# Token mix of the last 64 tokens of two batches on column halves of the array, and scores on the full array

## The chip, the cores and the metric

The kernel runs on one core of one Trainium2 chip. The metric is device microseconds of that core for one launch. Before the change the median of three runs is 381.34 us (381.15 to 381.44).

A short guide to the names: TensorE (PE in the profile; PEld is its weight load) multiplies a stationary operand `lhsT` with a moving operand `rhs` into PSUM. VectorE (DVE), ScalarE (ACT) and GpSimd (POOL) work element by element. Each engine takes its own instructions in program order and waits for others by semaphores.

## The reference

Eight batches of 576 tokens, 8 heads of 64 columns. Attention uses keys and values that are means over 8 neighbouring tokens, so there are 72 keys a head. A residual MLP follows, whose first half mixes the tokens of a batch with one 576 x 576 matrix.

```python
k_p = k.reshape(B, H, Sp, pool, D).mean(axis=3)          # Sp = 72, pool = 8
v_p = v.reshape(B, H, Sp, pool, D).mean(axis=3)
scores = scale * np.matmul(q, k_p.transpose(0, 1, 3, 2))  # 576 x 72 a head
attn = softmax(scores)                                    # exp, divided by its sum
attn_out = np.matmul(attn, v_p)
# ... heads side by side: x is (8, 576, 512)
a1 = alpha1 * x + beta1
tok = np.einsum('ts,bsd->btd', w_tok, a1)
u = x + lam * tok
a2 = alpha2 * u + beta2
ch = np.maximum(a2 @ w_ch1, 0.0) @ w_ch2                  # 512 -> 2048 -> 512
return u + lam * ch
```

## The kernel before

The 576 tokens of a batch are four chunks of 128 and a tail of 64. The tails of an even and an odd batch share one chunk `(b, 4)`: the even one in partitions 0 to 63, the odd one in 64 to 127. There are 36 chunks in all, and the MLP takes them in nine blocks of four. While block `n` runs its MLP, the attention and the token mix of batch `n + 1` are woven in: `todo` is a list of (position, action), sorted by position, where one step of the position is about one group of MLP matmuls.

Tiles in PSUM come from a pool of six (`gp`), with two more for the MLP's output:

```python
psA = ctx.enter_context(tc.tile_pool(name="psA", bufs=6, space=bass.MemoryType.PSUM))
psB = ctx.enter_context(tc.tile_pool(name="psB", bufs=2, space=bass.MemoryType.PSUM))

def gp(name):
    return psA.tile([P, 512], FP, tag="gp", name=name)
```

Keys and queries of two heads lie one above the other: head `2*hp` in partitions 0 to 63, head `2*hp + 1` in 64 to 127. The pooled keys are copied out of PSUM with one instruction:

```python
def att_K(b, u, copy):
    # ... matmuls into kp: 128 partitions x (2 pairs x 72 keys)
    copy(out=kpT_pool[u], in_=kp)
```

Scores of a pair, in two halves of 288 tokens. Each product contracts over 64 rows of the array; the two heads use its two halves. ScalarE takes the exponential of each into ET.

```python
def att_S(b, hp):
    st = st1[b]
    u, r = hp // 2, hp % 2
    for half in range(2):
        n0 = 288 * half
        both = [gp("ps_sc") for _ in range(2)]
        for hh in range(2):
            rows = slice(64 * hh, 64 * hh + 64)
            nc.tensor.matmul(out=both[hh][0:SPG, 0:288], lhsT=kpT_pool[u][rows, r, :],
                             rhs=st["qT"][u][rows, S * r + n0:S * r + n0 + 288])
        for hh in range(2):
            nc.scalar.activation(out=ET_pool[2 * r + hh][:, 64 + n0:64 + n0 + 288],
                                 in_=both[hh][0:SPG, 0:288],
                                 func=AF.Exp, bias=0.0, scale=0.125)
    # ...
```

`att_AV` multiplies ET with the pooled values (ps_av, five matmuls of 66 columns), and VectorE divides by the sums (`rec`, then x_tm). `att_X` scales x into the mix's operand xs:

```python
def att_X(b, h0, h1, eng=nc.vector):
    # ...
    eng.tensor_tensor(out=xs[:, 0:4, cols], in0=x[:, 0:4, cols],              # L388
                      in1=lamal_bc[:, cols]..., op=ALU.mult)
    p0 = 64 * (b % 2)
    eng.tensor_tensor(out=xs[p0:p0 + 64, 4, cols], in0=x[p0:p0 + 64, 4, cols],  # L392
                      in1=lamal_bc[p0:p0 + 64, cols], op=ALU.mult)
```

The token mix. A tail (`c == 4`) is computed like a full chunk: 128 output columns of which 64 are used, once for the even batch and once for the odd one.

```python
def mix_T(b, c, eng=nc.vector):
    key, s = chunk_of(b, c)
    p0, p1 = (0, P) if c < 4 else (64 * (b % 2), 64 * (b % 2) + 64)
    xs = xs_pool[b % 2]
    ps_tok = gp("ps_tok")
    t0 = P * c - 64 * (b % 2) if c == 4 else P * c
    for sc in range(5):
        kk, at = (P, sc) if sc < 4 else (P, 5) if b % 2 else (65, 4)
        nc.tensor.matmul(out=ps_tok, lhsT=wtT[0:kk, at, t0:t0 + P],
                         rhs=xs[0:kk, sc, :], start=(sc == 0), stop=(sc == 4))   # L422
    nc.vector.tensor_tensor(out=s["u"][p0:p1, :], in0=st1[b]["x"][p0:p1, c, :],  # L424
                            in1=ps_tok[p0:p1, 0:DM], op=ALU.add)
    eng.tensor_tensor(out=s["u_bf"][p0:p1, :], in0=s["u"][p0:p1, :],             # L426
                      in1=al2_bc[p0:p1, :], op=ALU.mult)
```

`mix_uT` (L437) then transposes u_bf on TensorE, and the MLP reads the result. The schedule of the attention of batch `b`, woven into block `b - 1`; GpSimd's casts and sums come first in it:

```python
def attention(b):
    late = b == 1
    todo = [(11.9 if late else -2.0, lambda: cast_rem(b, nc.gpsimd))]           # L107, L108
    for u in range(2):
        at = 10.0 + 4.8 * u if late else -1.0 + 6.6 * u
        todo.append((at, lambda u=u: cast_q(b, u, nc.gpsimd.tensor_copy)))      # L114
        todo.append((at + 0.1, lambda u=u: sum_k(b, u, nc.gpsimd)))             # L121, L122
        # ... att_F, att_V, att_Frem, att_K
    for h in range(8):
        at = 17.0 + 0.9 * h if late else 13.1 + 1.0 * h
        lag = 1.6 if late else 2.0
        if h % 2 == 0:
            todo.append((at, lambda h=h: att_S(b, h // 2)))
        todo.append((at + lag, lambda h=h: att_AV(b, h)))
        # ... att_X after every second head
    for c in range(5):
        at = 26.2 + 0.9 * c if late else 25.0 + c
        todo.append((at, lambda c=c: mix_T(b, c)))
        if c < 4 or b % 2:
            # ...
            todo.append((at + 1.8, lambda key=key: mix_uT(key)))
    return todo
```

In block 0 two of the MLP's output tiles (ps_ch2) are taken from the pool of six, and the tail of batch 0 is mixed at position 11.4 of that block.

Of the kernel before, what the change touches and what calls it, by code (L numbers as in the profile page):

```python
# [9 lines left out]
BF = mybir.dt.bfloat16  # L10
AF = mybir.ActivationFunctionType
ALU = mybir.AluOpType
AX = mybir.AxisListType

P = 128
SPG = 72
DM = 512
# [6 lines left out]
def kernel(  # L24
# [18 lines left out]
    nc = tc.nc  # L43
    ctx.enter_context(tc.manual_schedule())
    B, H, S, D = q.shape

    const = ctx.enter_context(tc.tile_pool(name="const", bufs=1))
# [4 lines left out]
    def gp(name):  # L52
        return psA.tile([P, 512], FP, tag="gp", name=name)
# [11 lines left out]
    st1 = {}  # L65
# [70 lines left out]
    al2_bc = const.tile([P, DM], FP, tag="al2_bc", name="al2_bc")  # L136
# [6 lines left out]
    start = const.tile([1, 2], FP, tag="start", name="start")  # L143
# [11 lines left out]
    for i, src in ((1, moe_alpha1), (0, moe_lam)):  # L155
        n = 65 if i in (0, 3) else 1
        nc.gpsimd.dma_start(out=vecs[0:n:64, i],
                            in_=src.unsqueeze(0).to_broadcast((1 + n // 65, DM)))
# [32 lines left out]
    vp1_pool, kpT_pool, ET_pool = [], [], []  # L191
    for i in range(4):
        t = const.tile([SPG, 2, 66], F16, tag=f"vp1_{i}", name=f"vp1_{i}")
        nc.vector.memset(t, 8.0)
        vp1_pool.append(t)
        if i < 2:
            kpT_pool.append(const.tile([P, 2, SPG], BF, tag=f"kpT_{i}", name=f"kpT_{i}"))
        t = const.tile([SPG, S + 128], F16, tag=f"ET_{i}", name=f"ET_{i}")
        nc.vector.memset(t[:, 0:64], 1.0)
        nc.vector.memset(t[:, 64 + S:], 1.0)  # L200
        ET_pool.append(t)
# [4 lines left out]
    xs_pool = [const.tile([P, 5, DM], BF, tag=f"xs_{i}", name=f"xs_{i}") for i in range(2)]  # L206
# [3 lines left out]
    wtT = const.tile([P, 6, 640], BF, tag="wtT", name="wtT")  # L210
# [112 lines left out]
    def att_K(b, u, copy):  # L323

        st = st1[b]
        ps_kp = gp("ps_kp")
        kp = ps_kp[:, 0:2 * SPG].rearrange("p (r g) -> p r g", g=SPG)
        for r in range(2):
            nc.tensor.matmul(out=kp[:, r, 0:64],
                             lhsT=st["k"][u][:, 2 * r:2 * r + 2].rearrange("p h d -> p (h d)"),  # L330
                             rhs=pool_main)
        nc.tensor.matmul(out=kp[:, :, 64:72], lhsT=st["rem"][1].rearrange("p h d -> p (h d)"),  # L332
                         rhs=pool_rem.rearrange("p (g u r) -> p u r g", r=2, u=2)[:, u])
        copy(out=kpT_pool[u], in_=kp)  # L334

    def att_V(b, hp):

# [4 lines left out]
        nc.vector.tensor_tensor(out=vp1_pool[hp][:, :, 0:64], in0=t[:, :, 0], in1=t[:, :, 1],  # L342
                                op=ALU.add)

    def att_S(b, hp):

        st = st1[b]
        u, r = hp // 2, hp % 2
        for half in range(2):
            n0 = 288 * half  # L350
            both = [gp("ps_sc") for _ in range(2)]
            for hh in range(2):
                rows = slice(64 * hh, 64 * hh + 64)
                nc.tensor.matmul(out=both[hh][0:SPG, 0:288], lhsT=kpT_pool[u][rows, r, :],  # L354
                                 rhs=st["qT"][u][rows, S * r + n0:S * r + n0 + 288])
            for hh in range(2):
                nc.scalar.activation(out=ET_pool[2 * r + hh][:, 64 + n0:64 + n0 + 288],  # L357
                                     in_=both[hh][0:SPG, 0:288],
                                     func=AF.Exp, bias=0.0, scale=0.125)
        for hh in range(2):  # L360
            st["ET"][2 * hp + hh] = ET_pool[2 * r + hh]

    def att_AV(b, h):
        st = st1[b]
        if "x" not in st:
            st["x"] = work.tile([P, 5, DM], FP, tag="x_tm", bufs=1, name="x_tm")
        hp, hh = h // 2, h % 2
        ET, vp1, x = st["ET"][h], vp1_pool[hp], st["x"]
        ps_av = gp("ps_av")
        av = ps_av[:, 0:5 * 66].rearrange("p (c x) -> p c x", x=66)  # L370
        for c in range(4):
            m0 = 64 + 64 * (hp % 2) + 128 * c
            nc.tensor.matmul(out=av[:, c, :], lhsT=ET[:, m0:m0 + 128],  # L373
                             rhs=vp1[:, hh, :])

        r0 = (64 if hp % 2 else 576) - 64 * (b % 2)
        nc.tensor.matmul(out=av[:, 4, :], lhsT=ET[:, r0:r0 + 128], rhs=vp1[:, hh, :])
        rec = work.tile([P, 5], FP, tag="rec", bufs=2, name="rec")
        nc.vector.reciprocal(out=rec, in_=av[:, :, 64:65])
        dd = D * h  # L380
        nc.vector.tensor_tensor(out=x[:, :, dd:dd + D], in0=av[:, :, 0:64],  # L381
                                in1=rec.unsqueeze(2).to_broadcast((P, 5, D)), op=ALU.mult)
# [16 lines left out]
    def chunk_of(b, c):  # L399
        key = (b, c) if c < 4 else (b - b % 2, 4)  # L400
        if key not in st2:
            st2[key] = {
                "u": work.tile([P, DM], FP, tag="u_sb", bufs=12, name="u_sb"),
                "u_bf": work.tile([P, DM], BF, tag="u_bf", bufs=4, name="u_bf"),
            }
        return key, st2[key]
# [6 lines left out]

    def mix_T(b, c, eng=nc.vector):
        key, s = chunk_of(b, c)
        p0, p1 = (0, P) if c < 4 else (64 * (b % 2), 64 * (b % 2) + 64)
        xs = xs_pool[b % 2]
        ps_tok = gp("ps_tok")
        t0 = P * c - 64 * (b % 2) if c == 4 else P * c
        for sc in range(5):  # L420
            kk, at = (P, sc) if sc < 4 else (P, 5) if b % 2 else (65, 4)
            nc.tensor.matmul(out=ps_tok, lhsT=wtT[0:kk, at, t0:t0 + P],  # L422
                             rhs=xs[0:kk, sc, :], start=(sc == 0), stop=(sc == 4))
        nc.vector.tensor_tensor(out=s["u"][p0:p1, :], in0=st1[b]["x"][p0:p1, c, :],  # L424
                                in1=ps_tok[p0:p1, 0:DM], op=ALU.add)
        eng.tensor_tensor(out=s["u_bf"][p0:p1, :], in0=s["u"][p0:p1, :],  # L426
                          in1=al2_bc[p0:p1, :], op=ALU.mult)

    def mix_uT(key):
        s = st2[key]  # L430
# [61 lines left out]
    for i, p0 in ((0, 64), (1, 0)):  # L492
        nc.vector.tensor_tensor(out=xs_pool[i][p0:p0 + 1, 4, :], in0=vecs[p0:p0 + 1, 3],
                                in1=vecs[p0:p0 + 1, 0], op=ALU.mult)
    cast_rem(0, nc.gpsimd, nc.vector.tensor_copy)
    att_Frem(0, (0,), nc.vector.tensor_copy)
    att_K(0, 0, nc.scalar.copy)
    for hp in range(2):
        att_S(0, hp)
    nc.vector.tensor_tensor(out=lamal_bc, in0=lamal_bc, in1=lam_bc, op=ALU.mult)  # L500
    load_wtok()
    att_V(0, 0)
# [16 lines left out]
    att_X(0, 2, 4)  # L519
    att_V(0, 2)  # L520
    att_V(0, 3)
    for hp in (2, 3):
        att_S(0, hp)
    att_AV(0, 4)
    att_AV(0, 5)
    setup_wtok(0, nc.scalar.copy)
    att_X(0, 4, 6, nc.gpsimd)
# [6 lines left out]
    setup_wtok(3, nc.scalar.copy)  # L534
    att_X(0, 6, 8)
    mix_T(0, 0, nc.gpsimd)
    setup_rowsum(2)
    setup_rowsum(3)
# [22 lines left out]
    def attention(b):  # L561


        late = b == 1
        todo = [(11.9 if late else -2.0, lambda: cast_rem(b, nc.gpsimd))]
# [3 lines that stand above are left out]
            todo.append((at + 0.1, lambda u=u: sum_k(b, u, nc.gpsimd)))  # L569
            for r in range(2):  # L570
                at = 12.7 + 4.6 * u + 1.6 * r if late else 2.7 + 6.6 * u + 2.4 * r
                hp = 2 * u + r
                todo.append((at, lambda hp=hp: att_F(b, hp)))
                todo.append((at + 0.5, lambda hp=hp: att_V(b, hp)))
                if r:
                    todo.append((at + 0.1, lambda u=u: att_Frem(b, (u,), nc.scalar.copy)))
                    todo.append((at + 0.4, lambda u=u: att_K(b, u, nc.vector.tensor_copy)))
        for h in range(8):
            at = 17.0 + 0.9 * h if late else 13.1 + 1.0 * h
            lag = 1.6 if late else 2.0  # L580
            if h % 2 == 0:
                todo.append((at, lambda h=h: att_S(b, h // 2)))
            todo.append((at + lag, lambda h=h: att_AV(b, h)))
            if h % 2:
                eng = nc.gpsimd if late and h < 5 else nc.vector
                todo.append((at + lag + 0.1, lambda h=h, eng=eng: att_X(b, h - 1, h + 1, eng)))
# [4 lines that stand above are left out]
                key = (b, c) if c < 4 else (b - 1, 4)  # L591
                todo.append((at + 1.8, lambda key=key: mix_uT(key)))
        return todo

    for n in range(NBLK):
        todo = []
        for j in range(0 if n else 4, NJ):
            todo.append((j, lambda j=j: mlp_A(n, j)))
        for m in range(4):
            for part in range(4):  # L600
                at = 16 + (4 * m + part if n else 4 * part + m)
# [9 lines left out]
        b = n + 1  # L611
        if b < B:
            todo += attention(b)
            if b + 1 < B:
                new_batch(b + 1)
                for u in range(2):
                    at = 20.0 + 0.2 * u if b == 1 else 0.4 + 1.0 * u
                    todo.append((at, lambda b=b, u=u: load_qk(b + 1, u)))
                    at = 22.0 + 0.2 * u if b == 1 else 5.8 + 6.6 * u
# [34 lines left out]
```

## Time and profile before

| | |
|---|---|
| time, median of three | 381.34 us |
| span of the profiled run | 379.6 us |
| mean granted TensorE clock | 0.995 |
| TensorE busy | 354.6 us, 93% |
| VectorE busy | 221.5 us, 58% |
| ScalarE busy | 184.5 us, 49% |
| GpSimd busy | 77.7 us, 20% |
| HBM | 38.04 MB read, 9.44 MB written |

How to read the lines that follow. A line of the page's shares gives busy time, share of the span and instructions of an engine. The chain is followed back from the last instruction to what released it, and shares say where its time lies. A line of the timeline gives the start and the length in microseconds of a run of like instructions, the engine, the line of the kernel, the operation, what is written from what, rows and columns of the array for a matmul ("64*72" is 64 rows, 72 columns), the shape, and how many; in brackets is the idle time of the engine before it and what ended it. Matmuls are pipelined: the next starts before the one before it has ended, so what one costs in a stream is the distance between starts.

### The profile page before, as it was taken

To read this page: it belongs to the slowest core of one execution; us is meant where nothing else is said; L and a number is where in the kernel's file an instruction comes from. 1 tells how busy PE (TensorE), PEld (TensorE's weight loads), DVE (VectorE), ACT (ScalarE), POOL (GpSimd) and SP (SyncE) were. 2 spreads that over 40 slices of the span, in tenths; PEclk is the share of its full clock that TensorE was granted. 3 is DMA by queue.
4 is the path that set the end of the run, shared out by engine and by line. 5 is a ranking of instruction groups with operands and counts; after the bars stand their busy time and mean duration, and the time that the engine had idled before them with its cause. 6 is when DMAs were issued, how large, how long until landed. Compare 5 with 4: busy or idle time off the path is not lost.

```text
span 379.6 us, 5854 instructions
## 1 busy us (share of the span) xinstructions
PE 354.6 (93%) x2241; PEld 185.7 (49%) x2283; DVE 221.5 (58%) x446; ACT 184.5 (49%) x380; POOL 77.7 (20%) x94
## 2 busy tenths in 40 slices
PE   2879999699999999999999999999999999999995
PEld 0365654245554555455545554555455544544542
DVE  4797756775596468736874688548754784011011
ACT  1574665117931693159415951586148603712710
POOL 7553432900700070007000700061000000000000
PEclk9999999989999999999999999999999999999999
DMA  8999999207631563147313732293110012002012
GB/s 201 223 200 214 262 238 253 49 29 242 154 90 58 169 173 90 57 139 201 90 57 121 219 92 56 75 264 86 40 50 1 3 54 57 0 29 83 1 48 65
DMA packets 34845, 43.02 MB, mean 113 GB/s; under 512 B 2360, under 2 KB 24956, under 8 KB 34816
## 3 DMA queue, kind: packets, MB, share of 16 engines
q1 hardware_dynamic: 31744, 37.76, 36.4%
q0 software_dynamic: 3072, 4.87, 7.3%
q8 instruction: 18, 0.29, 0.3%
q14 instruction: 11, 0.09, 0.1%
HBM read 38.04 MB, written 9.44 MB: 125 GB/s over the span
## 4 chain that ended last, share of the span: by engine, by line
PE 87%; DVE 7%; DMA 2%; issue 2%; POOL 1%; ACT 1%; POOLq 0%; DVEq 0%
PE ps_h L453 33%; PE ps_ch L471 32%; PE ps_tok L422 11%; PE ps_sc L354 3%; PE ps_uT L437 2%; DMA vecs<-in_moe_beta_dram 2%; PE ps_av L373 2%; PE ps_q L300 2%; DVE x_tm L381 1%; DVE v_u L340 1%; DVE xs L388 1%; DVE xs L392 1%; DVE u_sb L424 1%; DVE u_bf L426 1%; PE ps_bias L288 1%
## 5 line engine op out<-in xcount | busy, mean ns | idle before, releaser
L471 PE MATMUL ps_ch<-w,Hj 128*128 128x512 bf16 x555 | 137.7, 381 | 1.7 <-issue 0.8
L453 PE MATMUL ps_h<-u_fm,w 128*128 128x512 bf16 (+2 forms) x576 | 132.0, 374 | 0.9
L458 ACT ACTIVATE Hj<-ps_h,bias_cols 128x512 bf16<-128x512 f32 x144 | 97.9, 689 | 43.6 <-PE ps_h L453 42.7
L453 PEld LDWEIGHTS <-w 128*128 128x128 bf16 x592 | 63.6, 114 | 50.9 <-issue 1.6
L471 PEld LDWEIGHTS <-Hj 128*128 128x128 bf16 x576 | 51.3, 98 | 54.5 <-issue 6.8
L439 ACT COPY u_fm<-ps_uT 128x512 bf16<-128x512 bf16 x36 | 21.1, 585 | 99.7 <-PE ps_uT L437 99.6
L476 DVE TENSOR_TENSOR u_sb<-u_sb,ps_ch 128x512 f32<-128x512 f32 x36 | 24.5, 683 | 55.7 <-PE ps_ch L471 55.5
L422 PE MATMUL ps_tok<-xs,wtT 128*128 128x512 bf16 (+1 forms) x196 | 50.1, 385 | 3.7 <-DVE xs L388 3.2
L357 ACT ACTIVATE ET<-ps_sc 72x288 f16<-72x288 f32 x128 | 41.4, 412 | 19.2 <-PE ps_sc L354 19.0
L340 DVE TENSOR_TENSOR v_u<-v_u 72x512 f32<-72x512 f32 x64 | 43.8, 685 | 1.1
L424 DVE TENSOR_TENSOR u_sb<-x_tm,ps_tok 128x512 f32<-128x512 f32 (+1 forms) x40 | 27.5, 687 | 28.9 <-PE ps_tok L422 28.0
L107 POOL CAST rem_q<-rem_raw 128x256 bf16<-128x256 f32 x7 | 4.0, 565 | 142.9 <-DMA rem_raw<-in_q_dram 80.4
L381 DVE TENSOR_TENSOR x_tm<-ps_av,rec 128x320 f32<-128x320 f32 x64 | 31.5, 492 | 2.3
L422 PEld LDWEIGHTS <-wtT 128*128 128x128 bf16 (+1 forms) x200 | 19.4, 99 | 27.3 <-DVE xs L388 3.9
L334 DVE CAST kpT<-ps_kp 128x144 bf16<-128x144 f32 x14 | 4.3, 308 | 44.8 <-PE ps_kp L332 44.8
L426 DVE TENSOR_TENSOR u_bf<-u_sb,al_bc 128x512 bf16<-128x512 f32 (+1 forms) x38 | 26.9, 709 | 1.5
L121 POOL TENSOR_TENSOR qk_raw<-qk_raw 128x512 f32<-128x512 f32 x16 | 23.3, 1457 | 5.3 <-DMA qk_raw<-in_k_dram 5.3
L373 PEld LDWEIGHTS <-ET 72*128 72x128 f16 x256 | 16.4, 101 | 15.0 <-DVE vp L342 2.4
L388 DVE TENSOR_TENSOR xs<-x_tm,lamal_bc 128x512 bf16<-128x512 f32 x29 | 20.7, 714 | 0.9
L354 PE MATMUL ps_sc<-qT,kpT 64*72 64x288 bf16 x128 | 17.3, 313 | 2.6 <-ACT kpT L334 1.3
L373 PE MATMUL ps_av<-vp,ET 72*128 72x66 f16 x256 | 18.6, 199 | 0.9 <-ACT ET L357 0.8
L306 ACT COPY qT<-ps_q 128x512 bf16<-128x512 bf16 x32 | 18.4, 580 | 0.7 <-PE ps_q L300 0.7
(94 smaller groups left out, 233.8 us busy)
## 6 DMA issues: line engine op xcount, KB each, us to landing
qk_raw<-in_q_dram SPq DMA_DIRECT2D x16, 512.0 KB, 4.9
qk_raw<-in_k_dram SPq DMA_DIRECT2D x16, 512.0 KB, 6.9
v_u<-in_v_dram SPq DMA_DIRECT2D x16, 512.0 KB, 8.1
out_dram<-u_sb SPq DMA_DIRECT2D x32, 256.0 KB, 2.3
w<-in_moe_w_ch_dram POOLq DMA_DIRECT2D x8, 512.0 KB, 13.1
rem_raw<-in_q_dram SPq DMA_DIRECT2D x16, 64.0 KB, 9.1
rem_raw<-in_k_dram SPq DMA_DIRECT2D x16, 64.0 KB, 4.2
v_u<-in_v_dram SPq DMA_DIRECT2D x16, 64.0 KB
```

The lines of the kernel that those rows point to most:

```text
L340: nc.vector.tensor_tensor(out=t[:, :, 0:n], in0=t[:, :, 0:n], in1=t[:, :, n:2 * n], op=ALU.add)
L354: nc.tensor.matmul(out=both[hh][0:SPG, 0:288], lhsT=kpT_pool[u][rows, r, :], rhs=st["qT"][u][rows, S * r + n0:S * r + n0 + 288])
L357: nc.scalar.activation(out=ET_pool[2 * r + hh][:, 64 + n0:64 + n0 + 288], in_=both[hh][0:SPG, 0:288], func=AF.Exp, bias=0.0, scale=0.125)
L373: nc.tensor.matmul(out=av[:, c, :], lhsT=ET[:, m0:m0 + 128], rhs=vp1[:, hh, :])
L381: nc.vector.tensor_tensor(out=x[:, :, dd:dd + D], in0=av[:, :, 0:64], in1=rec.unsqueeze(2).to_broadcast((P, 5, D)), op=ALU.mult)
L422: nc.tensor.matmul(out=ps_tok, lhsT=wtT[0:kk, at, t0:t0 + P], rhs=xs[0:kk, sc, :], start=(sc == 0), stop=(sc == 4))
L424: nc.vector.tensor_tensor(out=s["u"][p0:p1, :], in0=st1[b]["x"][p0:p1, c, :], in1=ps_tok[p0:p1, 0:DM], op=ALU.add)
L426: eng.tensor_tensor(out=s["u_bf"][p0:p1, :], in0=s["u"][p0:p1, :], in1=al2_bc[p0:p1, :], op=ALU.mult)
L453: nc.tensor.matmul(out=ps_h[:, t0:t1], lhsT=w1_of(cc, j), rhs=u_fm[n][:, cc, t0:t1], start=(cc == 0), stop=(cc == 3))
L458: nc.scalar.activation(out=t, in_=ps_h, func=AF.Relu, bias=bias_cols[:, j:j + 1], scale=1.0)
L471: nc.tensor.matmul(out=ps, lhsT=Hj[n, j][:, 128 * m:128 * m + 128], rhs=w2[j // 4][:, j % 4, :], start=(j == 0), stop=(j == NJ - 1))
L476: nc.vector.tensor_tensor(out=u, in0=u, in1=ps, op=ALU.add)
```

## The change: tails side by side, scores by single heads

The mix of the tails waits for the odd batch. Then both tails are computed together: ten matmuls of 64 output columns each, the even batch's on columns (and PSUM partitions) 0 to 63, the odd one's on 64 to 127, alternating. One PSUM tile holds both, and one addition and one multiplication of full height replace two of half height. For the even batch only a copy of x's tail into u by GpSimd is left, since x is overwritten by the next batch; the odd batch copies its own half too.

The scores are no longer paired. The pooled keys of a pair lie in a tile with a place for each head whose other 64 rows are zero, so a product contracts over all 128 rows, of which the other head's queries meet zeros. Each head is scheduled for itself.

```diff
-            kpT_pool.append(const.tile([P, 2, SPG], BF, tag=f"kpT_{i}", name=f"kpT_{i}"))
+            t = const.tile([P, 2, 2, SPG], BF, tag=f"kpT_{i}", name=f"kpT_{i}")
+            nc.vector.memset(t, 0.0)
+            kpT_pool.append(t)
@@ att_K
-        copy(out=kpT_pool[u], in_=kp)
+        for hh in range(2):
+            rows = slice(64 * hh, 64 * hh + 64)
+            copy(out=kpT_pool[u][rows, hh], in_=kp[rows])
@@ att_S
-    def att_S(b, hp):
+    def att_S(b, h):
         st = st1[b]
-        u, r = hp // 2, hp % 2
+        u, r, hh = h // 4, h // 2 % 2, h % 2
+        ET = ET_pool[2 * r + hh]
         for half in range(2):
             n0 = 288 * half
-            both = [gp("ps_sc") for _ in range(2)]
-            for hh in range(2):
-                rows = slice(64 * hh, 64 * hh + 64)
-                nc.tensor.matmul(out=both[hh][0:SPG, 0:288], lhsT=kpT_pool[u][rows, r, :],
-                                 rhs=st["qT"][u][rows, S * r + n0:S * r + n0 + 288])
-            for hh in range(2):
-                nc.scalar.activation(...)
+            ps_sc = gp("ps_sc")
+            nc.tensor.matmul(out=ps_sc[0:SPG, 0:288], lhsT=kpT_pool[u][:, hh, r, :],
+                             rhs=st["qT"][u][:, S * r + n0:S * r + n0 + 288])
+            nc.scalar.activation(...)
@@ mix_T
-        p0, p1 = (0, P) if c < 4 else (64 * (b % 2), 64 * (b % 2) + 64)
-        xs = xs_pool[b % 2]
+        x = st1[b]["x"][:, c, :]
+        if c == 4:
+            rows = slice(64 * (b % 2), 64 * (b % 2) + 64)
+            nc.gpsimd.tensor_copy(out=s["u"][rows, :], in_=x[rows, :])
+            if b % 2 == 0:
+                return
+            x = s["u"]
         ps_tok = gp("ps_tok")
-        t0 = P * c - 64 * (b % 2) if c == 4 else P * c
         for sc in range(5):
-            kk, at = (P, sc) if sc < 4 else (P, 5) if b % 2 else (65, 4)
-            nc.tensor.matmul(out=ps_tok, lhsT=wtT[0:kk, at, t0:t0 + P],
-                             rhs=xs[0:kk, sc, :], start=(sc == 0), stop=(sc == 4))
-        nc.vector.tensor_tensor(out=s["u"][p0:p1, :], in0=st1[b]["x"][p0:p1, c, :],
-                                in1=ps_tok[p0:p1, 0:DM], op=ALU.add)
-        eng.tensor_tensor(out=s["u_bf"][p0:p1, :], in0=s["u"][p0:p1, :],
-                          in1=al2_bc[p0:p1, :], op=ALU.mult)
+            for odd in range(2) if c == 4 else (b % 2,):
+                kk, at = (P, sc) if sc < 4 else (P, 5) if odd else (65, 4)
+                m0, m = (64 * odd, 64) if c == 4 else (0, P)
+                nc.tensor.matmul(out=ps_tok[m0:m0 + m, :], lhsT=wtT[0:kk, at, P * c:P * c + m],
+                                 rhs=xs_pool[odd][0:kk, sc, :], start=(sc == 0), stop=(sc == 4))
+        nc.vector.tensor_tensor(out=s["u"], in0=x, in1=ps_tok, op=ALU.add)
+        eng.tensor_tensor(out=s["u_bf"], in0=s["u"], in1=al2_bc, op=ALU.mult)
@@ batch 0, second half of the heads
-    for hp in (2, 3):
-        att_S(0, hp)
+    for h in (4, 5, 6):
+        att_S(0, h)
     att_AV(0, 4)
+    att_S(0, 7)
     att_AV(0, 5)
@@ attention
-            if h % 2 == 0:
-                todo.append((at, lambda h=h: att_S(b, h // 2)))
+            todo.append((at, lambda h=h: att_S(b, h)))
```

More of the change, by code (lines that the diff above doesn't have):

```diff
@@ L343, in att_V @@
                                 op=ALU.add)
-    def att_S(b, hp):
+    def att_S(b, h):
         st = st1[b]
-        u, r = hp // 2, hp % 2
+        u, r, hh = h // 4, h // 2 % 2, h % 2
+        ET = ET_pool[2 * r + hh]
         for half in range(2):
             n0 = 288 * half
-            both = [gp("ps_sc") for _ in range(2)]
-            for hh in range(2):
-                rows = slice(64 * hh, 64 * hh + 64)
-                nc.tensor.matmul(out=both[hh][0:SPG, 0:288], lhsT=kpT_pool[u][rows, r, :],
-                                 rhs=st["qT"][u][rows, S * r + n0:S * r + n0 + 288])
-            for hh in range(2):
[L357 to L361, printed above, removed]
+            ps_sc = gp("ps_sc")
+            nc.tensor.matmul(out=ps_sc[0:SPG, 0:288], lhsT=kpT_pool[u][:, hh, r, :],
+                             rhs=st["qT"][u][:, S * r + n0:S * r + n0 + 288])
+            nc.scalar.activation(out=ET[:, 64 + n0:64 + n0 + 288], in_=ps_sc[0:SPG, 0:288],
+                                 func=AF.Exp, bias=0.0, scale=0.125)
+        st["ET"][h] = ET
     def att_AV(b, h):
@@ L497 @@
     att_K(0, 0, nc.scalar.copy)
-    for hp in range(2):
-        att_S(0, hp)
+    for h in range(4):
+        att_S(0, h)
     nc.vector.tensor_tensor(out=lamal_bc, in0=lamal_bc, in1=lam_bc, op=ALU.mult)
@@ L521 @@
     att_V(0, 3)
-    for hp in (2, 3):
-        att_S(0, hp)
+    for h in (4, 5, 6):
+        att_S(0, h)
     att_AV(0, 4)
+    att_S(0, 7)
     att_AV(0, 5)
```

## The prediction

> **What bounds the kernel now.** I read the page first: the shares of the engines and the chain that ended last.
>
> ```profile
> PE 354.6 (93%) x2241; PEld 185.7 (49%) x2283; DVE 221.5 (58%) x446; ACT 184.5 (49%) x380; POOL 77.7 (20%) x94
> PE 87%; DVE 7%; DMA 2%; issue 2%; POOL 1%; ACT 1%; POOLq 0%; DVEq 0%
> ```
>
> TensorE is busy 93% and makes 87% of the chain, so what counts is how long each piece holds its stream. A matmul's own duration (385 ns for a token-mix one) is no measure of that: matmuls overlap, and I take the distance between starts instead. I read it from the timeline of TensorE in a steady block.
>
> ```profile
> 177.71 0.38 PE L453 MATMUL ps_h<-u_fm,w 128*128 128x512 bf16 x1
> 178.02 0.44 PE L354 MATMUL ps_sc<-qT,kpT 64*72 64x288 bf16 x4
> 178.39 1.92 PE L453 MATMUL ps_h<-u_fm,w 128*128 128x512 bf16 x8
> ```
>
> The eight matmuls of the third line end 1.92 us after the first starts; taking off one's own 0.38 leaves 1.54 over seven, some 0.216 us each (one gap holds a little more). So 512 columns cost 0.216 us and, in proportion, 288 columns 0.123 us. The first matmul is followed after 0.31 us instead of 0.216: 0.09 us are lost on entering the form "64*72". The four score matmuls hold the stream for 0.37 us, where four one after the other would need 4 x 0.123 = 0.49. So the halves of the rows do run side by side (0.25 us for two rounds)[...].
>
> ```profile
> 160.80 1.24 PE L422 MATMUL ps_tok<-xs,wtT 128*128 128x512 bf16 x5
> 161.88 0.39 PE L437 MATMUL ps_uT<-identity_bf,u_bf 128*128 128x128 bf16 x4
> ```
>
> One mix of the last 64 tokens costs 161.88 - 160.80 = 1.08 us, the same as a mix of 128 tokens, although half of its columns serve nothing.
>
> Between blocks 1 and 6 I find almost no waits. The list of TensorE's waits has its entries before 77 us, so I laid out block 0, with the scores of batch 1 and its first mix.
>
> ```profile
> 63.02 0.31 PE L354 MATMUL ps_sc<-qT,kpT 64*72 64x288 bf16 x2
> 63.82 0.57 PE L354 MATMUL ps_sc<-qT,kpT 64*72 64x288 bf16 x2 [0.49 <-ACT ET L357]
> 69.47 1.27 DVE L388 TENSOR_TENSOR xs<-x_tm,lamal_bc 128x512 bf16<-128x512 f32 x1
> 70.16 1.71 POOL L121 TENSOR_TENSOR qk_raw<-qk_raw 128x512 f32<-128x512 f32 x1
> 70.76 1.26 DVE L392 TENSOR_TENSOR xs<-x_tm,lamal_bc 64x128 bf16<-64x128 f32 x1
> 74.25 1.04 PE L422 MATMUL ps_tok<-xs,wtT 128*128 128x512 bf16 x4 [2.67 <-DVE xs L388]
> 75.81 1.91 PE L471 MATMUL ps_ch<-w,Hj 128*128 128x512 bf16 x4
> ```
>
> Three things are to be seen. A pair asks for four PSUM buffers at once; the pool has six, and in block 0 two are held by the MLP's ps_ch2, so the second half waits for ScalarE's exponentials. Then the mix waits 2.67 us for VectorE. And after that wait four MLP matmuls take 1.91 instead of 1.03 us: the windows view gives a granted clock of 0.50 from 76 to 79 us. VectorE is late partly because GpSimd runs beside it: L392 takes 1.26 us there and 0.28 undisturbed; L388 1.27 and 0.68.
>
> [...] L392 above, begun at 70.76, ends at 72.02, just after L121 ended at 71.87. A VectorE instruction that reads PSUM (L381) took 0.49 us with and without GpSimd.
>
> **The change, part by part.**
>
> (1) Mix of the tails. Per pair of batches two runs of 1.08 us go, 2.16 us. In their place come ten matmuls on 64 columns. If they run two by two: five rounds of 0.22, plus entry and exit at 0.09 each (taken over from the row tiles) = 1.28 us. Gain 0.88 us per pair, on the path. Over pairs 1 to 3: 2.6 us. Pair 0 loses its early run (1.08 us in block 0) and has 1.28 - 1.08 = 0.2 us more at 83 us.
>
> (2) Scores. Per batch four bursts at 0.09 + 0.37 = 0.46, together 1.85 us, become 16 matmuls of 0.123 = 1.97 us: the full array with zeros does twice the work, but neither enters nor leaves a form. [...] some 0.2 us more per batch; six batches 1.2 us. Bursts that wait for PSUM buffers also in steady blocks (one per batch, about 0.08 us) give back 0.5. Net +0.7 us.
>
> (3) Scores come head by head and take two buffers, not four. Block 0's three waiting bursts hold TensorE for 1.11, 1.31 and 1.02 us from their first start to the next other matmul; a free one takes 0.37. Gain up to 2.3 us. With (1), TensorE reaches the last ps_av of batch 1 about 1.08 + 2.3 = 3.4, say 3.3 us earlier.
>
> (4) GpSimd gets a copy of the tail, x to u, ahead of the next batch's casts. An estimate from its casts (1024 columns 1.04 us, 256 columns 0.39): 0.6 us, eight times, off the path. But GpSimd works in order, and the copy waits until x is complete. The casts and sums of the next batch, 172.4 to 180.4 us in the steady block, move behind it, to about 190. In block 0 this frees L388 and L392 of heads 4 and 5 (2.53 to 0.96 us) [...]: VectorE's last stretch, 68.72 to 75.47, is shorter by about 1.0 us. The idle time of TensorE falls to some 1.7 us, and I give an even chance that the half clock (1.6 us) goes: 0.8.
>
> (5) The same move sets GpSimd's 7 us of work beside the mixes. Between the steady mix's u_bf (L426, two SBUF inputs, 0.69 us; L426 once took 1.35 beside a cast) and the transposes that need it there is little slack: L426 of the first chunk ends at 194.19, the transpose starts at 194.53. A sum of 1.26 us in the way costs up to 0.8 us on a chunk. Laying out two or three such meetings per batch, I get 0.4 to 0.9 us, say 0.7, for batches 1 to 6 (after batch 7 nothing is left to cast): +0.8 in block 0, +3.0 for the five others.
>
> (6) Two half copies of kpT in place of one: +0.3 us on VectorE (14 times) with TensorE elsewhere; at the start on ScalarE, where head 0 needs the first half only. One merged u_sb and u_bf per pair in place of two saves VectorE 1.4 us, off the path. Zeroing kpT falls into VectorE's 6.2 us wait at the start. I take +0.1.
>
> Sum: block 0: -3.3 - 1.0 - 0.8 + 0.2 + 0.8 = -4.1; steady: -2.6 + 0.7 + 3.0 = +1.1; start +0.1. Total -2.9, and 378.4; because (5) is the least sure and may cost less, I state 378.0 us.
>
> **Rivals.** *Column tiles do not overlap*: [...] 2.34 us per pair; 1.06 us lost against plan in each of four pairs, 382.2. For it: no column tile in this trace; against: the rows do it[...]. *No contention cost*: if GpSimd slips its work between VectorE's instructions, (5) falls out and the time is 374.2. For it: VectorE has free moments in every chunk (0.53 us before L424); against: L340 at 178.4 took 1.38 us instead of 0.42 beside L121. *VectorE binds block 0*: the 3.3 us that TensorE gains end in a longer wait at 74 us, leaving about 381. Against: VectorE idles some 4 us between 60 and 69, each time waiting for TensorE's ps_av or ps_kp. *Contention is worse*, 1.5 us a batch: 382.
>
> **Range and chances.** The rivals lie at 374.2 to 382.2, none likely together with another at the same end. I hold 374.3 to 381.3 with 8 in 10. 2% is 7.6 us: faster than 373.7 needs every gain and no contention, 0.07; slower than 389 would need a wait I don't see, 0.01; within, 0.92.
>
> **What would show it.** Right: ps_tok of chunk 4 as ten matmuls of 64 columns in about 1.28 us; ps_sc without a wait for ET in block 0; the first mix of batch 1 at about 70 rather than 74.25 us; GpSimd's L121 in the last quarter of a block, with L426 near 1.3 us and ps_uT waiting for it. Wrong: tails at 2.2 us or more, a mix still at 74, an L426 at 0.69 throughout, or scores at over 0.3 us a head.

## The result: 383.36 us, 0.6% slower

| | before | after |
|---|---|---|
| median, four runs each side by side | 381.25 us (380.46 to 381.44) | 383.36 us (383.31 to 384.15) |
| span of the profiled run | 379.6 us | 382.5 us |
| first scores of batch 2 start at | 100.6 us | 96.1 us |
| from there to the end | 279.1 us | 286.4 us |

The ratio is 1.0064, 95% interval 1.0045 to 1.0084. I had said 378.0 us (374.3 to 381.3). The last two rows, read from TensorE's timeline, show the shape of the error: up to the scores of batch 2 the change gained 4.5 us, where I had foreseen 4.0, and from there on it lost 7.3 us, where I had foreseen about 1.

The lines of the kernel have moved a little: in the changed kernel L391 is what L392 was, L387 L388, L430 L426, L427 L422, L440 L437, L356 L354. The page after, first the shares and the chain that ended last:

```profile
PE 352.1 (92%) x2241; PEld 191.0 (50%) x2283; DVE 226.1 (59%) x454; ACT 187.6 (49%) x382; POOL 86.3 (23%) x102
...
PE 68%; DVE 19%; DMA 8%; issue 3%; POOL 1%; SPq 0%; ACT 0%; DVEq 0%; POOLq 0%
```

TensorE's busy time fell by 2.5 us while the span rose by 2.9; in the chain VectorE went from 7 to 19%. DMA went from 2 to 8% there, but TensorE's list of waits has no DMA after the start. What TensorE waited for, after (total, times, longest, in us), of the list the lines of the mix:

```profile
PE ps_tok L427 <- DVE xs L391: 5.4, 3, 1.8
PE ps_uT L440 <- DVE u_bf L430: 3.7, 8, 0.6
```

Both stand at the mix; before, the first did not occur in the steady blocks and the second was 1.3 us, three times (once in each of batches 3, 5 and 7). The timeline after, at the start of the mix of batch 4: GpSimd, and between its lines the instruction of VectorE and the two of TensorE that matter:

```profile
188.41 1.13 POOL L418 COPY u_sb<-x_tm 64x512 f32<-64x512 f32 x1 [31.13 <-DVE x_tm L380]
188.99 3.66 DVE L391 TENSOR_TENSOR xs<-x_tm,lamal_bc 64x128 bf16<-64x128 f32 x1
189.49 0.39 POOL L107 CAST rem_q<-rem_raw 128x256 bf16<-128x256 f32 x1
189.85 0.45 POOL L108 TENSOR_TENSOR rem_k<-rem_raw 128x128 bf16<-128x128 f32 x1
189.88 1.03 PE L427 MATMUL ps_tok<-xs,wtT 128*128 128x512 bf16 x4
190.25 1.03 POOL L114 CAST q_bf<-qk_raw 128x1024 bf16<-128x1024 f32 x1
191.25 1.25 POOL L121 TENSOR_TENSOR qk_raw<-qk_raw 128x512 f32<-128x512 f32 x1
...
192.58 0.72 POOL L122 TENSOR_TENSOR k_bf<-qk_raw 128x256 bf16<-128x256 f32 x1
...
192.70 0.38 PE L427 MATMUL ps_tok<-xs,wtT 65*128 65x512 bf16 x1 [1.80 <-DVE xs L391]
```

A multiplication of 64 x 128 elements, 0.28 us alone, takes 3.66 us. It stands there while GpSimd runs the rest of its copy and then four more instructions, and ends at 192.65: 0.15 us after the end of L121, 0.07 after the start of L122. The last matmul of the mix waits for it: from 189.88 to 192.70 are 2.82 us, four matmuls take 4 x 0.216, so 1.96 us of TensorE are lost.

### The profile page after: what moved, and what is told of

It is laid out like the page before. It is cut to its first block, busy times and chain, and to the rows that moved or that the text cites. A ratio compares the mean times of both kernels' runs of the same rounds, so it can differ in the third digit from the quotient of the medians.

```text
span 382.5 us, 5900 instructions
## 1 busy us (share of the span) xinstructions
PE 352.1 (92%) x2241; PEld 191.0 (50%) x2283; DVE 226.1 (59%) x454; ACT 187.6 (49%) x382; POOL 86.3 (23%) x102
## 4 chain that ended last, share of the span: by engine, by line
PE 68%; DVE 19%; DMA 8%; issue 3%; POOL 1%; SPq 0%; ACT 0%; DVEq 0%; POOLq 0%
PE ps_h L456 29%; PE ps_ch L474 23%; PE ps_tok L427 8%; DVE xs L391 3%; DVE x_tm L380 3%; DMA v_u<-in_v_dram 3%; PE ps_sc L356 3%; DMA rem_raw<-in_q_dram 3%; DVE u_sb L429 2%; DVE u_bf L430 2%; DVE xs L387 2%; DMA vecs<-in_moe_beta_dram 2%; PE ps_uT L440 2%; DVE v_u L344 1%; PE ps_q L302 1%
## 5 line engine op out<-in xcount | busy, mean ns | idle before, releaser
L358 ACT ACTIVATE ET<-ps_sc 72x288 f16<-72x288 f32 x128 | 44.8, 407 | 21.0 <-PE ps_sc L356 21.0
L427 PE MATMUL ps_tok<-xs,wtT 128*128 128x512 bf16 (+3 forms) x197 | 44.7, 380 | 6.9 <-DVE xs L391 5.4
L418 POOL COPY u_sb<-x_tm 64x512 f32<-64x512 f32 x8 | 8.3, 1039 | 186.3 <-DVE x_tm L380 186.3
L344 DVE TENSOR_TENSOR v_u<-v_u 72x512 f32<-72x512 f32 x64 | 36.6, 572 | 11.7 <-DMA v_u<-in_v_dram 10.1
L338 DVE CAST kpT<-ps_kp 64x144 bf16<-64x144 f32 x28 | 8.5, 305 | 42.0 <-PE ps_kp L334 41.7
L430 DVE TENSOR_TENSOR u_bf<-u_sb,al_bc 128x512 bf16<-128x512 f32 x34 | 29.7, 874 | 1.2
L356 PE MATMUL ps_sc<-qT,kpT 128*72 128x288 bf16 x128 | 28.1, 308 | 2.6 <-ACT kpT L338 1.3
L427 PEld LDWEIGHTS <-wtT 128*128 128x128 bf16 (+3 forms) x200 | 17.3, 100 | 22.3 <-DVE xs L387 1.5
L429 DVE TENSOR_TENSOR u_sb<-x_tm,ps_tok 128x512 f32<-128x512 f32 x32 | 21.9, 683 | 9.6 <-PE ps_tok L427 9.6
L121 POOL TENSOR_TENSOR qk_raw<-qk_raw 128x512 f32<-128x512 f32 x16 | 23.4, 1461 | 6.2 <-DMA qk_raw<-in_k_dram 6.2
L387 DVE TENSOR_TENSOR xs<-x_tm,lamal_bc 128x512 bf16<-128x512 f32 x29 | 20.3, 700 | 0.9
L391 DVE TENSOR_TENSOR xs<-x_tm,lamal_bc 64x128 bf16<-64x128 f32 x29 | 19.7, 679 | 0.3
```

The source lines that it names most:

```text
L344: nc.vector.tensor_tensor(out=t[:, :, 0:n], in0=t[:, :, 0:n], in1=t[:, :, n:2 * n], op=ALU.add)
L356: nc.tensor.matmul(out=ps_sc[0:SPG, 0:288], lhsT=kpT_pool[u][:, hh, r, :], rhs=st["qT"][u][:, S * r + n0:S * r + n0 + 288])
L358: nc.scalar.activation(out=ET[:, 64 + n0:64 + n0 + 288], in_=ps_sc[0:SPG, 0:288], func=AF.Exp, bias=0.0, scale=0.125)
L427: nc.tensor.matmul(out=ps_tok[m0:m0 + m, :], lhsT=wtT[0:kk, at, P * c:P * c + m], rhs=xs_pool[odd][0:kk, sc, :], start=(sc == 0), stop=(sc ...
L429: nc.vector.tensor_tensor(out=s["u"], in0=x, in1=ps_tok, op=ALU.add)
L430: eng.tensor_tensor(out=s["u_bf"], in0=s["u"], in1=al2_bc, op=ALU.mult)
```

## The experiments

All keep the full computation. Times are medians; the "before" beside them was 380.9 to 381.1 us. In each profile I split the span at the first scores of batch 2, which separates block 0 from the steady blocks. Two things blur the column "first scores of batch 2": TensorE ran at half clock for 3.4 us of block 0, some 1.6 us lost, in five of these profiles (before, copy on ScalarE, casts ahead of the copy, new scores alone, new tails alone: a granted clock of 0.50 to 0.52 in the lowest window of 2 or 3 us between 73 and 79 us) and in none of the others (1.00 from 70 to 82 us), and block 0 does not begin at the same time in all of them (36.4 to 37.4 us, its first ps_h). The clock also differs between runs of one kernel: of the new tails alone, four with a mean granted clock of 0.999 or 1.0 took 377.75 to 378.11 us, thirteen with 0.994 or 0.995 took 378.64 to 380.00.

| kernel | median, us | ratio to before (95%) | first scores of batch 2 | from there to the end |
|---|---|---|---|---|
| before | 381.25 | | 100.6 | 279.1 |
| after | 383.36 | 1.0064 (1.0045 to 1.0084) | 96.1 | 286.4 |
| copy on ScalarE | 377.62 | 0.9919 (0.9891 to 0.9947) | 98.8 | 278.3 |
| casts ahead of the copy | 378.30 | 0.9913 (0.9883 to 0.9944) | 98.6 | 278.4 |
| before, with a bare copy | 388.11 | 1.0183 (1.0137 to 1.0230) | 97.4 | 289.2 |
| new scores alone | 377.57 | 0.9923 (0.9897 to 0.9949) | 98.1 | 279.1 |
| new tails alone, copy on ScalarE | 379.09 | 0.9955 (0.9940 to 0.9970) | 99.8 | 278.3 |
| after, first sum of keys first | 378.34 (one run) | | 96.6 | 280.0 |
| copy on ScalarE, later transposes | 373.30 | 0.9787 (0.9727 to 0.9846) | 96.7 | 274.8 |
| mixed order of casts, later transposes | 372.61 | 0.9763 (0.9708 to 0.9819) | 96.1 | 274.9 |
| new scores alone, later transposes | 376.92 | 0.9902 (0.9870 to 0.9935) | 96.9 | 277.4 |

### Is it the order in GpSimd's queue? Two ways to undo it

Theory A: the copy is put into GpSimd's queue ahead of the next batch's casts, and cannot start until x is complete. It drags them into the mix, where L391 and L430 of VectorE are held beside them. Rival B: the new matmuls themselves cost more than I thought. Rival C: it is the copy's own run.

```diff
-            nc.gpsimd.tensor_copy(out=s["u"][rows, :], in_=x[rows, :])
+            nc.scalar.copy(out=s["u"][rows, :], in_=x[rows, :])
```

> The changed kernel with the copy of x's tail on ScalarE instead of GpSimd, nothing else. Theory A (in GpSimd's queue the copy waits for the finished x and holds the next batch's casts behind it[...]): the stalls of about 1.95 us in even batches and 1.06 us in odd ones go, three and two times, while block 0 gets some contention back: 376 us (375 to 378), L121 back near the middle of a block, L391 at 0.28 us. Theory B (the loss lies in the tail's column form or in the padded scores themselves): no change, 383 us.

Measured 377.62 us. The timeline of this kernel, GpSimd's first instruction for the next batch and VectorE's last L391 ahead of the mix, in the same block:

```profile
170.38 0.40 POOL L107 CAST rem_q<-rem_raw 128x256 bf16<-128x256 f32 x1 [30.81 <-DMA rem_raw<-in_q_dram]
...
188.66 0.28 DVE L391 TENSOR_TENSOR xs<-x_tm,lamal_bc 64x128 bf16<-64x128 f32 x1
```

The casts are back at 170 us, L391 at 0.28. The other way leaves the copy on GpSimd and moves the casts ahead of it:

```diff
+                at = 28.0 if b == 1 else 24.0
+                todo.append((at, lambda b=b: cast_rem(b + 1, nc.gpsimd)))
+                for u in range(2):
+                    todo.append((at + 0.1, lambda b=b, u=u: cast_q(b + 1, u, nc.gpsimd.tensor_copy)))
+                    todo.append((at + 0.2, lambda b=b, u=u: sum_k(b + 1, u, nc.gpsimd)))
# and the same three taken out of attention(b) for b > 1
```

> The changed kernel, copy still on GpSimd, but the next batch's casts and sums are put into the program ahead of it (position 24 of the block before, 28 in block 0). Theory A: the order alone matters, not who copies: 376 us (375 to 378). Theory B: 383 us. Theory C (it is the copy's own 1.04 us on GpSimd that disturbs VectorE): still above 381 us.

Measured 378.30 us, 0.3 above what A allowed, with 278.4 us after batch 2's scores where the copy on ScalarE had 278.3. Here GpSimd copies for 1.13 us as before, and TensorE's list of waits has none for L391 (5.4 us in the changed kernel), so B and C are out: it is what the copy holds up.

### The wait alone, added to the kernel before

```diff
+        if c == 4:
+            nc.gpsimd.tensor_copy(out=spare[p0:p1, :], in_=st1[b]["x"][p0:p1, c, :])
```

> The kernel before, with nothing but a copy of x's tail by GpSimd into a tile that nobody reads, at each mix of a tail. Theory A: it brings the whole loss without any of the change: stalls of 1 to 2 us in each of batches 2 to 6, less what block 0 gains from later casts: 386 to 389 us. Theories B and C: at most 1.5 us more than before, 381 to 383 us.

Measured 388.11 us: a copy that nobody reads costs 7 us. In even batches it shows the same picture; in its timeline, TensorE's lines of the mix:

```profile
190.62 1.03 PE L426 MATMUL ps_tok<-xs,wtT 128*128 128x512 bf16 x4
193.72 0.38 PE L426 MATMUL ps_tok<-xs,wtT 65*128 65x512 bf16 x1 [2.08 <-DVE xs L392]
```

By starts 2.24 us are lost here (193.72 - 190.62 less 4 x 0.216), 6.7 us in the three even batches. The windows view gives a granted clock of 0.79 from 190 to 198 us, which makes 3.4 us of half the TensorE clock, some 1.6 us lost; after the first wait, from 110 to 116 us, it is 1.00. The mean over the span, 0.989 where the changed kernel has 0.997, makes some 3.1 us, two such stretches by this estimate; with the 6.7 us that is nearly all of the 10.1 us by which this kernel is slower from batch 2's scores on. The waits of 1.80 us in the changed kernel were not followed by half clock: 1.00 from 112 to 120, from 190 to 198 and from 268 to 276 us. In odd batches nothing is lost here: L392 takes 0.59 us, and TensorE waits for u_bf as in the kernel before (1.3 us, three times). I had expected stalls there too, so this run shows the loss of the even batches alone; that of the odd ones rests on the two ways to undo the order.

### Each part by itself

The new scores with the old mix:

```diff
# before.py with the changed kpT tile, att_K, att_S and schedule of the scores; mix_T as before
```

> The kernel before with the new scores (padded keys, head by head) and the old mix. Theory A: some 0.1 us more per batch in the stream, and block 0 gains about 2 us from its freed PSUM buffers: 379 to 381 us. Theory B with the scores at fault: 384 us or more.

Measured 377.57 us, faster than I had said by 1.4 to 3.4 us. In the profiles all of it lies in block 0 (98.1 instead of 100.6 us, both with half clock; three of the four runs, with a mean granted clock of 0.999 to 1.0 instead of 0.995, took about 377.5); from there on the two kernels take the same 279.1 us. So scores on the full array with half the rows zero cost no more than the pairs did. TensorE's timeline of block 0 in this kernel, scores of the third and fourth head:

```profile
59.55 0.20 PE L376 MATMUL ps_av<-vp,ET 72*128 72x66 f16 x1
59.58 0.41 PE L356 MATMUL ps_sc<-qT,kpT 128*72 128x288 bf16 x2
59.94 0.38 PE L302 MATMUL ps_q<-identity_bf,q_bf 128*128 128x128 bf16 x4
...
61.46 0.41 PE L356 MATMUL ps_sc<-qT,kpT 128*72 128x288 bf16 x2
61.71 1.03 PE L470 MATMUL ps_ch<-w,Hj 128*128 128x512 bf16 x3
```

Two products hold the stream for 0.25 us (61.46 to 61.71), start 0.03 us after the last ps_av, without the 0.09 us on entry, and wait for no buffer.

The new tails with the old scores, copy on ScalarE so that the queue is left alone:

```diff
# before.py with the changed mix_T; att_S and the rest as before
+            nc.scalar.copy(out=s["u"][rows, :], in_=x[rows, :])
```

> The kernel before with the tails in columns alone, copy on ScalarE, scores in pairs as before. Theory: per pair 0.88 us less in the stream, less 0.58 us of the wait at chunk 3 in even batches, and about 1 us for the tail that leaves block 0: 379.5 us (378.5 to 380.5). Rival (the tails' form does nothing here and all gain of the copy on ScalarE is the scores'): 381 us.

Measured 379.09 us: 0.8 us come in block 0, 0.8 after it. In block 0 the two parts do not add: with both and the copy on ScalarE batch 2 is scored at 98.8, with the new scores alone at 98.1, all with half clock.

### Where the stream time of the tails went

```diff
-                todo.append((at + 1.8, lambda key=key: mix_uT(key)))
+                last = c == (4 if b % 2 else 3) and not late
+                todo.append((at + (2.7 if last else 1.8), lambda key=key: mix_uT(key)))
```

> The changed kernel with the copy on ScalarE, and the last transpose of each batch from 2 on (chunk 3 of an even batch, the tails' chunk of an odd one) 0.9 positions later, behind one more MLP group. Theory: the tail's column form has saved TensorE 0.9 us a pair, but in even batches the old tail mix had covered VectorE's way to u_bf of chunk 3; a wait of 0.58 us stands there now, as it always did in odd batches. With the transposes later six waits of 0.56 to 0.58 us go: 3.4 us less than the copy on ScalarE alone, 374.2 us (373.5 to 375). Rival (that time is not a wait for u_bf but TensorE's own, or comes back elsewhere): 377 to 378 us.

Measured 373.30 us; from batch 2's scores to the end 274.8 instead of 278.3 us, 3.5 less where 3.4 were foreseen; its list of waits has none for u_bf left. TensorE's timeline of the changed kernel at the end of an even batch:

```profile
199.24 0.39 PE L440 MATMUL ps_uT<-identity_bf,u_bf 128*128 128x128 bf16 x4
199.46 1.03 PE L474 MATMUL ps_ch<-w,Hj 128*128 128x512 bf16 x4
200.91 0.40 PE L440 MATMUL ps_uT<-identity_bf,u_bf 128*128 128x128 bf16 x4 [0.42 <-DVE u_bf L430]
```

and with the transpose one group later:

```profile
193.90 1.89 PE L474 MATMUL ps_ch<-w,Hj 128*128 128x512 bf16 x8
195.63 0.39 PE L440 MATMUL ps_uT<-identity_bf,u_bf 128*128 128x128 bf16 x4
```

In the kernel before, the mix of the tail stood where the first of these shows 0.42 us of idle time (by starts: 200.91 - 199.46 less four matmuls of 0.216, so 0.58 us lost). TensorE's timeline before, at the end of the same batch:

```profile
199.95 1.24 PE L422 MATMUL ps_tok<-xs,wtT 128*128 128x512 bf16 x5
201.04 0.39 PE L437 MATMUL ps_uT<-identity_bf,u_bf 128*128 128x128 bf16 x4
```

To see that the columns have their own share, I gave the new scores with the old mix the same later transposes (in batches 3, 5 and 7, where they waited):

```diff
+                last = c == 4 and not late
+                todo.append((at + (2.7 if last else 1.8), lambda key=key: mix_uT(key)))
```

> The kernel before with the new scores and the old mix, and the tails' transpose of batches 3, 5 and 7 0.9 positions later. It is the later transposes without the tails in columns. Theory: three waits of 0.58 us go, 1.7 us less than the new scores alone (377.2 us in its profile), so 375.5 us; the copy on ScalarE with later transposes (371.6 in its profile, 373.3 median) is then some 3 us faster, the stream time that the columns save. From the scores of batch 2 to those of batch 7 this kernel should take 192.1 us, that one took 189.3. Rival (the later transposes alone bring it, the columns nothing): 373.5 us and 190 us.

From the scores of batch 2 to those of batch 7 it takes 192.1 us and the kernel with columns 189.3: both as said, so the columns do bring 2.8 us up to there, and 2.6 us to the end (277.4 and 274.8). The medians, 376.92 and 373.30, agree; the first is 1.4 above my number, with runs from 375.3 to 378.1.

### When a waiting VectorE instruction gets in

```diff
-            todo.append((at + 0.1, lambda u=u: sum_k(b, u, nc.gpsimd)))
+            todo.append((at + 0.1 if late or u else -2.1, lambda u=u: sum_k(b, u, nc.gpsimd)))
```

The theory, read from the timeline after: the waiting L391 is let in where GpSimd's queue has a gap, and the gap lies ahead of L122, which needs the result of L121.

> The changed kernel with the first sum of keys (L121, then L122 on its result) at the head of GpSimd's queue behind the copy, in place of third. [...] L391 in even batches takes about 1.9 us instead of 3.66, being let in after the first L121, and the mix's wait for it falls from 1.8 us to below 0.3. Rival (the two engines take turns, and L391 was held for another reason): L391 keeps its 3.6 us, or falls to below 1 us.

The same work on GpSimd, still behind the copy, in another order. Its timeline, both engines:

```profile
186.60 1.13 POOL L418 COPY u_sb<-x_tm 64x512 f32<-64x512 f32 x1 [29.99 <-DVE x_tm L380]
187.18 1.92 DVE L391 TENSOR_TENSOR xs<-x_tm,lamal_bc 64x128 bf16<-64x128 f32 x1
187.69 1.25 POOL L121 TENSOR_TENSOR qk_raw<-qk_raw 128x512 f32<-128x512 f32 x1
...
189.03 0.72 POOL L122 TENSOR_TENSOR k_bf<-qk_raw 128x256 bf16<-128x256 f32 x1
```

L391 takes 1.92 us, as said, and ends once more 0.07 us after the start of L122; TensorE's wait for it is gone from the list, and the one run took 378.34 us. GpSimd pauses there: 0.09 us from the end of L121 to the start of L122, which needs its result, while the independent ones before it follow with no pause (after: 189.49 + 0.39 to 189.85).

But a pause is not the only way in. Some 1.2 us after L391 has ended in the changed kernel, another VectorE instruction is held:

```profile
193.25 1.03 POOL L114 CAST q_bf<-qk_raw 128x1024 bf16<-128x1024 f32 x1
193.88 0.95 DVE L430 TENSOR_TENSOR u_bf<-u_sb,al_bc 128x512 bf16<-128x512 f32 x1
194.25 1.72 POOL L121 TENSOR_TENSOR qk_raw<-qk_raw 128x512 f32<-128x512 f32 x1
```

L121 follows L114 with no pause, and yet L430 gets in between: it ends at 194.83, 0.55 us after L114, and L121 takes 1.72 us instead of 1.25. The same happens with L430 at 153.86 (1.48 us, and L121 1.72) and, with the first sum first, at 192.23 (1.25 us, and L121 1.71). So the pause fits L391 in these two orders, and does not tell why L391 had to pass four changes of instruction where L430 needed one.

### A version that beats both

Casts of batches 3 to 7 ahead of the copy, those of batch 2 behind it, and the later transposes:

```diff
-                at = 28.0 if b == 1 else 24.0
+                at = 31.9 if b == 1 else 24.0
```

> As before this, but with the copy on GpSimd: the casts of batches 3 to 7 ahead of the copy, those of batch 2 behind it, as in the changed kernel. Theory: behind the copy they leave VectorE free at the end of block 0 (2 us less up to batch 2's scores in the changed kernel than with the copy on ScalarE), ahead of it they leave it free in the later mixes; with the later transposes: 372 us (371 to 373.5). Rival (the order in block 0 makes no difference of its own): 374 to 375 us.

Measured 372.61 us, 2.4% (1.8 to 2.9) below the kernel before. Of the 2 us that I expected from the order in block 0 only about 0.6 show (96.1 against 96.7 us; 0.9 counted from the start of block 0), in one profile each, and the runs of the two kernels overlap (372.50 to 373.04, 372.79 to 374.88): that this order has a gain of its own is not shown. Most of what I had seen there was the clock: the profile of the copy on ScalarE alone has 3.4 us at half clock from 73 us on, the one with later transposes none, though both run the same program in block 0.

## Why the prediction was wrong, point by point

**(1) The tails' stream time was right, its worth was not.** TensorE's timeline after, a tails' mix of an odd batch:

```profile
158.34 0.81 PE L474 MATMUL ps_ch<-w,Hj 128*128 128x512 bf16 x3
159.08 1.27 PE L427 MATMUL ps_tok<-xs,wtT 128*64 128x512 bf16 x10
160.28 0.40 PE L440 MATMUL ps_uT<-identity_bf,u_bf 128*128 128x128 bf16 x4
```

Ten matmuls in 1.20 us from first start to the next instruction, and 0.09 on entry: 1.29 us against 1.28 foreseen. So the column tiles overlap (ten in a row at 0.216 us would take 2.16), and entering costs the same 0.09 us as for rows (159.08 - 158.34 less three times 0.216). Of the 1.20 us five rounds at 0.216 make 1.08; for the 0.12 left I had put 0.09 as an exit, by estimate, and what they consist of is not shown. The failing step is "on the path": the mix of the even tail, 1.08 us, had also covered VectorE's way to u_bf of chunk 3. Without it 0.58 us of wait stand there in batches 2, 4 and 6, so 1.7 of the 2.6 us were given back. The profile before had shown that latency where no tail mix follows, in the odd batches, and I had read past it when I wrote that TensorE's waits end before 77 us:

```profile
163.56 0.40 PE L437 MATMUL ps_uT<-identity_bf,u_bf 128*128 128x128 bf16 x4 [0.42 <-DVE u_bf L426]
```

**(2) Scores: +0.7 us foreseen, 0.0 measured** (279.1 us with either form). Of the 0.2 us more a batch, 0.09 were for weights behind a short ps_av, a guess of mine that no trace had shown; they do not show here either: a head takes 0.25 us (61.46 to 61.71 above), eight of them 2.0. Against the 1.93 us that I had for the bursts with their wait that leaves 0.07 us a batch, some 0.4 us in six; what makes up for it stays open.

**(3) Freed buffers, and the whole of block 0: the sum came out, by luck.** -4.1 us foreseen, and +0.1 for the start; 4.5 measured up to batch 2's scores. But TensorE reaches the last ps_av of batch 1 at 68.82 us instead of 69.66, 0.8 us earlier and not 3.3. Counted from the start of block 0, which came 0.4 us later, it is 1.2 us, and 1.1 of these are the tail's mix that left: the freed buffers gave about 0.2 us, not up to 2.3. Two heads still wait for ScalarE's exponentials, which I had named as gone; TensorE's timeline after:

```profile
61.20 0.28 PE L356 MATMUL ps_sc<-qT,kpT 128*72 128x288 bf16 x1 [0.49 <-ACT ET L358]
...
65.03 0.28 PE L356 MATMUL ps_sc<-qT,kpT 128*72 128x288 bf16 x1 [0.49 <-ACT ET L358]
```

With the new scores alone these waits are absent, and the same stretch is 1.7 us shorter than before; why they return with the tails is not shown. What was missing came from elsewhere: from the last ps_av to the first mix 1.7 us instead of 1.0 (the mix starts at 71.7 us instead of 74.25; I had said about 70), the half clock, counted at half its 1.6 us, did not come at all, and of the 0.8 us of contention nothing shows between the first mix and batch 2's scores.

**(4) Where GpSimd's work goes: right.** I put the start of the moved casts at about 190 us; it was 189.49. The copy took 0.60 us only in block 0 (at 49.7 us), beside VectorE 1.06 to 1.13.

**(5) What it costs there: this step failed.** I laid it out as meetings in turns, VectorE held for one GpSimd instruction at most, "a sum of 1.26 us in the way", 0.7 us a batch (which makes 3.5 us in five batches; I wrote 3.0). L391 was held by the copy and four more in a row, in each of batches 2, 4 and 6, and TensorE lost about 1.95 us each time. I had named L391 (L392 in the prediction) only for block 0. In odd batches L391 got through and L430 was held instead, by one instruction each time as I had laid it out; VectorE's timeline of such a batch, after, with TensorE's mix of chunk 1 and the transposes of chunk 0 behind it:

```profile
149.16 0.59 DVE L391 TENSOR_TENSOR xs<-x_tm,lamal_bc 64x128 bf16<-64x128 f32 x1
...
151.41 1.24 PE L427 MATMUL ps_tok<-xs,wtT 128*128 128x512 bf16 x5
151.47 1.76 DVE L430 TENSOR_TENSOR u_bf<-u_sb,al_bc 128x512 bf16<-128x512 f32 x1
153.28 0.40 PE L440 MATMUL ps_uT<-identity_bf,u_bf 128*128 128x128 bf16 x4 [0.63 <-DVE u_bf L430]
...
153.86 1.48 DVE L430 TENSOR_TENSOR u_bf<-u_sb,al_bc 128x512 bf16<-128x512 f32 x1
...
156.57 1.26 DVE L430 TENSOR_TENSOR u_bf<-u_sb,al_bc 128x512 bf16<-128x512 f32 x1
```

TensorE lost 0.8 us ahead of the transposes of chunk 0 and 0.26 ahead of those of chunk 2 (from the start of the mix to that of the transposes, less 1.08). Three times 1.95 and twice 1.06 make 8.0 us instead of 3.0. With the tails' -2.6 and the exposed wait's +1.7 that is 7.1, against 7.3 measured.

So it was the rival "contention is worse, 1.5 us a batch: 382" that came, at 1.6 us a batch (8.0 in five), with the exposed wait on top (1.5 us in the five steady batches and the rest of my sum make 382.5). That its number comes near 383.36 is partly chance, since it was meant as longer meetings at u_bf, and three quarters of the loss came at xs. I had put the edge of the range at 381.3, below my own rival.

## What to carry to other kernels

When an instruction is added to an engine that runs far ahead of the others, ask what stands behind it in that engine's queue: one wait moves all of it to a later time, beside other neighbours. When a piece of a full engine's work is taken out, ask which other latency it was covering, and move the next consumer by that much. And where an instruction takes longer beside another engine's (here 3.66 us instead of 0.28), do not take the length of one of these as the longest wait: here one instruction waited through five of the other engine's, others through one.

## What I had not expected of the hardware

A waiting VectorE instruction did not get in at the next change of GpSimd's instruction each time. I had laid it out so that one instruction's length, 1.25 us here, was the longest wait. Measured is 3.66 us, through five GpSimd instructions in all, and 1.92 us when the dependent pair came first; both ended just behind the pause between L121 and L122 (0.08 and 0.09 us). That the pause lets L391 in fits both runs; I did not lengthen or remove the pause itself, and L430 got in without one (above), so that the pause decides is not shown. Why L391 got in behind the copy in odd batches (0.59 us) and not in even ones stays open: the copy took 1.06 us there instead of 1.13, and L107 started 0.07 us after its end instead of 0.05 before. With the casts ahead of the copy TensorE did not wait for L391 in even batches.

Half clock did not follow from such a wait alone: with waits of about 2.1 us at the first mix of batch 1 it came for 3.4 us in the copy on ScalarE (granted clock 0.50 from 74 to 76 us) and did not in the same stretch of the kernel with later transposes (1.00).
